# Shared weight loads, 16-head softmax groups, x stationary and TensorE in written order in a decode attention kernel

## The chip, the cores and the metric

One core of one Trainium2 chip. The metric is the device time of one execution in microseconds (us), median of several executions; "span" is the profiled execution without its fixed start and end, 1.6 to 1.8 us shorter. In the profiles, PE is TensorE's matmuls and PEld its weight loads (the weights are a matmul's stationary operand), DVE is VectorE, ACT is ScalarE, POOL is GpSimd and SP is SyncE, which here only issues transfers. "Clock" is the share of TensorE's full clock that was granted. `A <- B` in a list of waits means that A waited for B; `[0.30 <-B]` in a timeline means that the engine had been idle for 0.30 us, until B ended.

## The reference

```python
def reference(A_x, A_k_cache, A_v_cache, A_wq, A_wo, B_x, B_w_r, B_w_gate, B_w_up, B_w_down, gate_w):
    x = A_x                                          # (4, 1, 1024) bf16
    g = sigmoid((x * gate_w).sum(-1, keepdims=True))
    q = (x @ wq) as (4, 32 heads, 1, 128)
    p = softmax(q @ k_cache^T * 128 ** -0.5)         # k_cache, v_cache: (4, 32, 8192, 128) bf16
    a = (p @ v_cache) as (4, 1, 4096) @ wo
    b = x + sigmoid(x @ w_r) * ((silu(x @ w_gate) * (x @ w_up)) @ w_down)   # S = 1: the selection picks the only row
    return g * a + (1 - g) * b
```

(Shortened; the shapes are those of the inputs.) The K and V caches are 537 MB of the 576 MB that must be read.

## The kernel before

Each "piece" is 4 MB of K or V, or up to 4 MB of weights, loaded into one slot of a ring of five. Each K piece holds two heads and has four chunks; a chunk is transposed by DVE into one of two T buffers and then read by eight matmuls. A V piece feeds 32 matmuls. (In the code below and in the diffs, comments are added.)

```python
    ring = ctx.enter_context(tc.tile_pool(name="ring", bufs=5))
    ttp = ctx.enter_context(tc.tile_pool(name="ttp", bufs=2))      # the two T buffers
    ptp = ctx.enter_context(tc.tile_pool(name="ptp", bufs=2))
    # ... (cut)
    def add_x():                                    # adds (1 - g) * x into the output's accumulator
        xb = ptp.tile([Bn, D], BF, name="xb", bufs=1)
        nc.sync.dma_start(out=xb[:], in_=x2)
        xf = ptp.tile([Bn, D], F32, name="xf", bufs=1)
        nc.vector.tensor_copy(out=xf[:], in_=xb[:])
        for n in range(NH):
            mm_acc(acc[:, n * NB:(n + 1) * NB], dg[:], xf[:, n * NB:(n + 1) * NB])
    # ... (cut)
    def k_piece(u):
        # ... (cut)
        kn = slot()
        nc.sync.dma_start(out=kn[:], in_=kv_view(A_k_cache, u))
        for c in range(JR // CJ):
            T = ttp.tile([P, CJ, 2, 32, 2], BF, name="T", tag="T")
            nc.vector.transpose(out=T[:]...bitcast(U32), in_=kn[:, c * CJ * Dh:(c + 1) * CJ * Dh].bitcast(U32))
            for jl in range(CJ // 16):
                # ... (cut)
                for he in range(4):
                    nc.tensor.matmul(sps[:, :], lhsT=Z[:, he, s:s + P], rhs=T[:, 16 * jl:16 * jl + 16, half, :, e], ...)
            if c == 0:
                flush()
        if t == GT - 1:
            softmax(g)                              # GT = 4 pieces, 8 heads
    # ... (cut)
    for kind, u in order:                           # k 0, k 1, ..., then k u and v u - LAG in turn
        if kind == "k":
            k_piece(u)
        # ... (cut)
        if (kind, u) == ("k", NT // 2):             # NT // 2 = 32
            add_x()
```

Of the kernel before, what the change touches and what calls it, by code (L numbers as in the profile page):

```python
# [9 lines left out]
BF = mybir.dt.bfloat16  # L10
# [5 lines left out]
PSUM = bass.MemoryType.PSUM  # L16


@with_exitstack
def kernel(  # L20
# [21 lines left out]

    nc = tc.nc
# [8 lines left out]
    GT = 4  # L52
    GH = GT * HT
    NQ = 4
# [3 lines left out]
    LAG = 4  # L58
# [6 lines left out]
    assert JR == 128 and JC * GT == 32 and H % GH == 0 and D % NB == 0  # L65
# [7 lines left out]
    ptp = ctx.enter_context(tc.tile_pool(name="ptp", bufs=2))  # L73
    stat = ctx.enter_context(tc.tile_pool(name="stat", bufs=3))
    shrp = ctx.enter_context(tc.tile_pool(name="shrp", bufs=1, space=PSUM))
    accp = ctx.enter_context(tc.tile_pool(name="accp", bufs=1, space=PSUM))
    scp = ctx.enter_context(tc.tile_pool(name="scp", bufs=2, space=PSUM))
    ops = ctx.enter_context(tc.tile_pool(name="ops", bufs=2, space=PSUM))
    o2p = ctx.enter_context(tc.tile_pool(name="o2p", bufs=1, space=PSUM))

# [5 lines left out]
    x6 = const.tile([NX, D], BF)  # L86
# [5 lines left out]
    shr = shrp.tile([P, 512], F32)  # L92
    nc.vector.memset(shr[:], 0.0)
# [4 lines left out]
    xw_ps = o2p.tile([P, DT, NX], BF, name="xw", tag="oT")  # L98
# [7 lines left out]
    for he in range(4):  # L106
# [6 lines left out]
                            base=0, pattern=[[-JC, GT], [-32, NQ]], channel_multiplier=1)  # L113
    nc.gpsimd.affine_select(out=m32[:], in_=m32[:], compare_op=ALU.is_ge, fill=0.0,
                            base=JC - 1, pattern=[[JC, GT], [32, NQ]], channel_multiplier=-1)
# [6 lines left out]
    selg = const.tile([P, 4, GT, HT], F32)  # L122
    nc.gpsimd.memset(selg[:], 0.0)
    nc.gpsimd.affine_select(out=selg[:], in_=selg[:], compare_op=ALU.not_equal, fill=1.0,
                            base=0, pattern=[[-1, 4], [-32, GT], [-4, HT]], channel_multiplier=1)
    OS = [const.tile([P, 4 * Dh], F32, name=f"OS{i}") for i in range(2)]
    ZW = 31 + P + 1
    Zt = [const.tile([P, 4, ZW], BF, name=f"Z{i}") for i in range(2)]
    PB = [const.tile([P, 32, 4, HT, 4], BF, name=f"PB{i}") for i in range(2)]
    for z in Zt + PB + OS:  # L130
        nc.gpsimd.memset(z[:], 0.0)

    qT = const.tile([P, H, Bn], BF)
# [7 lines left out]
    FT = FG * FR  # L141
    o0 = 0
    gu_ps = shr[:, o0:o0 + 2 * FT * Bn].rearrange("p (w g r b) -> p w g r b", w=2, g=FG, r=FR); o0 += 2 * FT * Bn
    q_ps = shr[:, o0:o0 + H * Bn].rearrange("p (h b) -> p h b", h=H); o0 += H * Bn
    rg_ps = shr[:, o0:o0 + 2 * Bn].rearrange("p (w b) -> p w b", w=2); o0 += 2 * Bn
    assert o0 <= 512
    acc = accp.tile([Bn, D], F32)

# [6 lines left out]
    def gates():  # L155
        wrep = ttp.tile([P, 2, DT, P], BF, name="wrep", tag="T")
        for i in range(2):
            nc.vector.tensor_copy(out=wrep[:, i, :, :], in_=xw[:, :, Bn + i:Bn + i + 1].to_broadcast([P, DT, P]))
            for t in range(DT):
                mm_acc(rg_ps[:, i, :], wrep[:, i, t, :], xT[t])  # L160
        nc.scalar.activation(out=sgb[:], in_=rg_ps, func=ACT.Sigmoid)
# [4 lines left out]
    def add_x():  # L166
        xb = ptp.tile([Bn, D], BF, name="xb", bufs=1)
        nc.sync.dma_start(out=xb[:], in_=x2)
        xf = ptp.tile([Bn, D], F32, name="xf", bufs=1)
        nc.vector.tensor_copy(out=xf[:], in_=xb[:])  # L170
        for n in range(NH):
            mm_acc(acc[:, n * NB:(n + 1) * NB], dg[:], xf[:, n * NB:(n + 1) * NB])
# [8 lines left out]

    def wq_piece(t0):
        w = slot()[:, :TW * H * Dh].rearrange("p (t h d) -> p t h d", t=TW, h=H)
        nc.sync.dma_start(out=w.rearrange("p t h d -> p t (h d)"), in_=wqv[:, t0:t0 + TW, :])
        for t in range(TW):
            for h in range(H):
                mm_acc(q_ps[:, h, :], w[:, t, h, :], xT[t0 + t])

    def q_done():
        nc.vector.tensor_copy(out=qT[:], in_=q_ps)  # L190
        qa_ps = ops.tile([P, 4, H * Bn], F32, name="o_ps")
# [5 lines left out]
    def gu_piece(view, w_i, t0):  # L197
        w = slot()[:, :TW * F].rearrange("p (t g f r) -> p t g f r", t=TW, g=FG, r=FR)
        nc.sync.dma_start(out=w.rearrange("p t g f r -> p t (g f r)"), in_=view[:, t0:t0 + TW, :])
        for t in range(TW):  # L200
            for g in range(FG):
                for r in range(FR):
                    mm_acc(gu_ps[:, w_i, g, r, :], w[:, t, g, :, r], xT[t0 + t])

    def h_done():
        g_sb = stat.tile([P, FT, Bn], F32, tag="g_sb", bufs=1)
        fl = lambda ap: ap.rearrange("p g r b -> p (g r) b")
        nc.scalar.activation(out=g_sb[:], in_=fl(gu_ps[:, 0]), func=ACT.Silu)
# [60 lines left out]
    def k_piece(u):  # L269
# [3 lines left out]
        for a in range(NQ):  # L273
            nc.gpsimd.tensor_copy(out=Z[32 * a:32 * a + 32, :, 31 + 32 * a:32 + 32 * a],  # L274
# [160 lines left out]
```

## Time and profile before

| | before |
|---|---|
| time, median | 1351.3 us (1351.1 to 1351.8) |
| span | 1349.5 us |
| PE, PEld, DVE busy | 1066, 434, 623 us |
| data moved | 576.5 MB, mean 427 GB/s |

From the page of the kernel before: the span in 40 slices (busy tenths of PE and DVE, of the 16 DMA engines, and the rate of the transfers), the instruction queue (packets, MB, share), and the median time from issue to landing of a K piece.

```profile
PE   2775887888788877879788887879877787887878
DVE  1553445444553555355355435535553454455500
DMA  9999999999999999999999999999999999999997
GB/s 398 436 431 424 432 430 429 431 434 432 429 432 432 432 427 432 433 432 429 431 434 431 429 430 435 432 428 432 430 434 425 434 434 432 429 428 435 433 421 321
...
q8 instruction: 40, 0.66, 0.2%
...
piece<-in_A_k_cache_dram SPq DMA_DIRECT2D x64, 4096.0 KB, 37.4
```

DMA is at nine tenths or more in all slices but the last, whatever PE and DVE do. A piece lands 37.4 us after its issue, and 4 MB at 431 GB/s (an inner slice) take 9.7 us: nearly four pieces are typically queued. While that is so, idle PE or DVE costs nothing.

From the timeline of the same run, SP alone (start, duration, what): the issues around the middle, where the 8 KB of `x` for the residual (`xb`) are loaded.

From the timeline (start, duration, what): the last chunk of a K piece and a V piece on PE, and the end of the run.

```profile
641.22 1.90 PE L290 MATMUL S_ps<-T,Z_140 128*128 128x512 bf16 x8 [0.30 <-DVE T L283]
643.05 7.07 PE L346 MATMUL o_ps<-piece,PB_142 128*8 128x512 bf16 x32
...
1342.79 3.77 PE L150 MATMUL acc<-piece,LT 128*4 128x512 bf16 x16 [0.68 <-DMA piece<-in_A_wo_dram]
```

After the last piece of `wo` has landed there are 16 matmuls, a cast and the store. (One such matmul is shown as 0.38 us long when alone, yet 16 end within 3.77 us: matmuls overlap. This matters below.)

### The profile page before, as it was taken

How to read it: one execution, taken by the hardware profiler on the slowest of the kernel's cores; microseconds unless marked ns; L12 is line 12 of the kernel's file. 1: busy time of each engine (PE TensorE's matmuls, PEld its weight loads, DVE VectorE, ACT ScalarE, POOL GpSimd, SP SyncE). 2: the span in 40 equal slices, each digit the busy share in tenths (PEclk: the TensorE clock that was granted, in tenths of full speed). 3: DMA queues.
4: the chain of work that ended last, by engine and by line, in shares of the span. 5: the costliest groups of instructions: out<-in, count | busy, mean ns of one | idle time of the engine just before them, and what ended most of it. 6: DMA issues, size and time to landing. Idle time of an engine off the chain costs nothing.

```text
span 1349.5 us, 11806 instructions
## 1 busy us (share of the span) xinstructions
PE 1066.2 (79%) x5112; PEld 434.1 (32%) x5112; DVE 622.5 (46%) x403; ACT 71.0 (5%) x118; POOL 86.3 (6%) x326
## 2 busy tenths in 40 slices
PE   2775887888788877879788887879877787887878
PEld 2332333333233333323333333333333332333333
DVE  1553445444553555355355435535553454455500
ACT  0001000000000000000000000000000000000000
POOL 2000000000000000000000000000000000000000
PEclk9877998889898888979999888999989889998999
DMA  9999999999999999999999999999999999999997
GB/s 398 436 431 424 432 430 429 431 434 432 429 432 432 432 427 432 433 432 429 431 434 431 429 430 435 432 428 432 430 434 425 434 434 432 429 428 435 433 421 321
DMA packets 22040, 576.46 MB, mean 427 GB/s; under 512 B 2386, under 2 KB 2394, under 8 KB 2660
## 3 DMA queue, kind: packets, MB, share of 16 engines
q1 hardware_dynamic: 21968, 575.69, 99.4%
q8 instruction: 40, 0.66, 0.2%
q14 instruction: 12, 0.10, 0.0%
q10 hardware_dynamic: 20, 0.02, 0.0%
HBM read 575.69 MB, written 0.01 MB: 427 GB/s over the span
## 4 chain that ended last, share of the span: by engine, by line
DMA 48%; PE 32%; DVE 12%; issue 6%; POOL 2%; ACT 1%; DVEq 0%; SPq 0%; ACTq 0%
DMA piece<-in_A_k_cache_dram 42%; PE o_ps L346 16%; PE S_ps L290 14%; DVE T L283 10%; DMA piece<-in_A_v_cache_dram 5%; DMA piece<-in_A_wo_dram 1%; PE oT L359 1%; PE acc L150 1%; DVE PT L315 1%; PE shr L150 1%; POOL PB_142 L320 1%; POOL PB_143 L320 1%; POOL tot L324 0%; ACT OS_138 L352 0%; ACT OS_139 L352 0%
## 5 line engine op out<-in xcount | busy, mean ns | idle before, releaser
L283 DVE STREAM_TRANSPOSE T<-piece 128x2048 uint32<-128x2048 uint32 x256 | 576.2, 2288 | 455.9 <-DMA piece<-in_A_k_cache_dram 367.7
L290 PE MATMUL S_ps<-T,Z_140 128*128 128x512 bf16 x1024 | 288.9, 437 | 158.4 <-DVE T L283 158.1
L290 PE MATMUL S_ps<-T,Z_141 128*128 128x512 bf16 x1024 | 260.0, 402 | 81.5 <-DVE T L283 81.4
L346 PE MATMUL o_ps<-piece,PB_143 128*8 128x512 bf16 x1024 | 229.5, 383 | 4.6 <-DMA piece<-in_A_v_cache_dram 4.6
L346 PE MATMUL o_ps<-piece,PB_142 128*8 128x512 bf16 x1024 | 226.2, 379 | 4.1 <-DMA piece<-in_A_v_cache_dram 4.1
L290 PEld LDWEIGHTS <-Z_140 128*128 128x128 bf16 x1024 | 111.3, 109 | 332.5 <-issue 252.5
L290 PEld LDWEIGHTS <-Z_141 128*128 128x128 bf16 x1024 | 102.4, 101 | 237.9 <-issue 142.2
L346 PEld LDWEIGHTS <-PB_143 128*8 128x8 bf16 x1024 | 87.1, 87 | 143.2 <-issue 17.7
L346 PEld LDWEIGHTS <-PB_142 128*8 128x8 bf16 x1024 | 86.4, 87 | 141.6 <-issue 12.8
L362 DVE SCALAR_TENSOR_TENSOR OT<-oT,sgb,rinv 128x8 bf16<-128x8 f32 x16 | 3.8, 236 | 147.5 <-PE oT L359 147.5
L274 POOL COPY Z_141<-qa 32x4 bf16<-32x4 bf16 x128 | 24.9, 195 | 517.3 <-PE S_ps L290 511.8
L274 POOL COPY Z_140<-qa 32x4 bf16<-32x4 bf16 x128 | 24.9, 195 | 499.1 <-PE S_ps L290 485.1
L352 ACT COPY OS_138<-o_ps 8x512 f32<-8x512 f32 x32 | 18.5, 577 | 568.6 <-PE o_ps L346 568.6
L352 ACT COPY OS_139<-o_ps 8x512 f32<-8x512 f32 x32 | 18.5, 577 | 548.8 <-PE o_ps L346 548.8
L150 PE MATMUL shr<-xw,piece 128*128 128x4 bf16 x704 | 22.6, 170 | 2.8 <-DMA piece<-in_A_wq_dram 2.6
L150 PEld LDWEIGHTS <-piece 128*128 128x128 bf16 x704 | 22.6, 113 | 3.9 <-DMA piece<-in_A_wq_dram 2.7
L326 DVE RECIPROCAL rinv<-tot 128x8 f32<-128x8 f32 x16 | 3.2, 203 | 25.6 <-POOL tot L324 25.6
L150 PE MATMUL acc<-piece,LT 128*4 128x512 bf16 x64 | 14.5, 378 | 0.7 <-DMA piece<-in_A_wo_dram 0.7
L359 PE MATMUL oT<-selg,OS_139 128*128 128x8 f32 x64 | 8.5, 259 | 5.7 <-ACT OS_139 L352 5.7
L359 PE MATMUL oT<-selg,OS_138 128*128 128x8 f32 x64 | 8.5, 259 | 5.7 <-ACT OS_138 L352 5.7
L150 PE MATMUL acc<-piece,hT 128*4 128x512 bf16 x56 | 12.4, 379 | 0.0
L313 ACT ACTIVATE PTs<-S_ps,negm 128x512 bf16<-128x512 f32 x16 | 11.0, 688 | 25.8 <-DVE negm L310 25.4
(99 smaller groups left out, 142.5 us busy)
## 6 DMA issues: line engine op xcount, KB each, us to landing
piece<-in_A_k_cache_dram SPq DMA_DIRECT2D x64, 4096.0 KB, 37.4
piece<-in_A_v_cache_dram SPq DMA_DIRECT2D x63, 4096.0 KB, 36.2
piece<-in_A_wq_dram SPq DMA_DIRECT2D x2, 4096.0 KB, 22.6
piece<-in_B_w_gate_dram SPq DMA_DIRECT2D x2, 3584.0 KB, 39.9
piece<-in_B_w_up_dram SPq DMA_DIRECT2D x2, 3584.0 KB, 33.6
piece<-in_A_wo_dram SPq DMA_DIRECT2D x7, 1024.0 KB, 19.9
piece<-in_B_w_down_dram SPq DMA_DIRECT2D x1, 4096.0 KB, 39.7
piece<-in_A_v_cache_dram SPq DMA_DIRECT2D x4, 1024.0 KB, 31.7
```

The lines of the kernel that those rows point to most:

```text
L150: nc.tensor.matmul(out_ap, lhsT=lhsT, rhs=rhs, start=start, stop=True, skip_group_check=True)
L274: nc.gpsimd.tensor_copy(out=Z[32 * a:32 * a + 32, :, 31 + 32 * a:32 + 32 * a], in_=qa[32 * a:32 * a + 32, :, h0 + a // QH, b:b + 1])
L283: nc.vector.transpose(out=T[:].rearrange("p j h i e -> p (j h i e)").bitcast(U32), in_=kn[:, c * CJ * Dh:(c + 1) * CJ * Dh].bitcast(U32))
L290: nc.tensor.matmul(sps[:, :], lhsT=Z[:, he, s:s + P], rhs=T[:, 16 * jl:16 * jl + 16, half, :, e], start=(t == 0 and jc == 0 and he == 0), ...
L313: nc.scalar.activation(out=PTs[:], in_=sps[:], func=ACT.Exp, bias=negm[:, 0:1], scale=scale, accum_out=rs[:, 0:1])
L315: nc.vector.transpose(out=PT[:].rearrange("p j i -> p (j i)"), in_=PTs[:])
L320: nc.gpsimd.tensor_copy(out=B_[W:P, :, :, 1, :], in_=Pv[W:P])
L326: nc.vector.reciprocal(out=rinv[:], in_=tot[:])
L346: nc.tensor.matmul(o_ps[32 * t:32 * t + NM, :], lhsT=B_[:, JC * t + jc, uq].rearrange("p s j -> p (s j)"), rhs=vn[:, j0 * Dh:(j0 + 4) * Dh ...
L352: nc.scalar.copy(out=o_sb[32 * t:32 * t + NM, :], in_=o_ps[32 * t:32 * t + NM, :])
L359: nc.tensor.matmul(oT[:, :], lhsT=o_sb[:, q * Dh:(q + 1) * Dh], rhs=selg[:, q].rearrange("p t s -> p (t s)"), start=(q == 0), stop=(q == 3))
L362: nc.vector.scalar_tensor_tensor(out=OT[:, hg:hg + GH, b], in0=oT[:, :], scalar=sgb[:, 1, b:b + 1], in1=rinv_t.pop(g)[:], op0=ALU.mult, op ...
```

## The change

The intent: order the matmuls so that two in a row use the same weights, and drop the second weight load; form softmax groups of 16 heads (8 pieces) instead of 8, so that the pairs exist; compute q, gate and up with x as the stationary operand; keep TensorE's instructions in written order, so that pairs stay together. The larger tiles need room, so several small tiles move into other tiles' buffers. The core of the diff:

```diff
+def keep_weights(nc):        # drops a weight load equal to the one held, if it carries no wait or update
+    ...
-    GT = 4
+    GT = 8
-    LAG = 4
+    LAG = GT
-    ptp = ctx.enter_context(tc.tile_pool(name="ptp", bufs=2))
+    ptp = ctx.enter_context(tc.tile_pool(name="ptp", bufs=1))
-    scp = ctx.enter_context(tc.tile_pool(name="scp", bufs=2, space=PSUM))
+    scp = ctx.enter_context(tc.tile_pool(name="scp", bufs=1, space=PSUM))     # scores: one buffer, two banks
+    ctx.enter_context(tc.manual_schedule(engines={mybir.EngineType.PE}))
+    nc.at_finalize(keep_weights)
... (cut)
     def add_x():
-        xb = ptp.tile([Bn, D], BF, name="xb", bufs=1)
-        nc.sync.dma_start(out=xb[:], in_=x2)
-        xf = ptp.tile([Bn, D], F32, name="xf", bufs=1)
-        nc.vector.tensor_copy(out=xf[:], in_=xb[:])
+        xs = ttp.tile([Bn, 3 * D], BF, name="xs", tag="T")
+        xb, xf = xs[:, 0:D], xs[:, D:3 * D].bitcast(F32)
+        nc.sync.dma_start(out=xb, in_=x2)
+        nc.vector.tensor_copy(out=xf, in_=xb)
... (cut: q, gate and up with x stationary and transposes after them)
-            for jl in range(CJ // 16):
-                jc = c * (CJ // 16) + jl
-                s = 31 - (JC * t + jc)
-                for he in range(4):
-                    half, e = divmod(he, 2)
-                    nc.tensor.matmul(sps[:, :], lhsT=Z[:, he, s:s + P], rhs=T[:, 16 * jl:16 * jl + 16, half, :, e], ...)
+            s = 31 - (JT * t + c)
+            for he in range(4):
+                half, e = divmod(he, 2)
+                for z in range(2):
+                    nc.tensor.matmul(sps[:, z, :], lhsT=Z[:, he, s:s + P], rhs=T[:, 16 * z:16 * z + 16, half, :, e], ...)
... (cut: V likewise, pairs of matmuls with one weight load; eviction of four V pieces at a time by ACT and DVE)
     last += [wo_block(NWB - 1, 0, FR - 1), wo_block(NWB - 1, FR - 1, FR)]
+    last.pop(0)()
     flush()
+    last.pop(0)()
     o_rows(GE, NWB)
```

More of the change, by code (lines that the diff above doesn't have):

```diff
@@ L16 @@
 PSUM = bass.MemoryType.PSUM
+def keep_weights(nc):
+    for f in nc.m.functions:
+        for block in f.blocks:
+            held, kept, alone = None, [], False
+            for i in block.instructions:
+                if i.engine == mybir.EngineType.PE:
+                    if isinstance(i, mybir.InstLdweights):
+                        a, y = i.ins[0], i.sync_info
+                        key = (a.memref, a.offset, str(a.ap), str(a.dtype), i.tile_size, i.tile_position, i.is_transpose)
+                        free = y is None or not (y.on_wait or y.on_update)
+                        if free and held == key:
+                            continue
+                        held = key
+                    elif not isinstance(i, mybir.InstMatmult) or i.ldweights is not False:
+                        held = None
+                kept.append(i)
+            block.instructions = kept
 @with_exitstack
@@ L51 @@
     JC = JR // 16
-    GT = 4
+    GT = 8
+    JT = JC // 2
+    RT = 4
     GH = GT * HT
+    RH = RT * HT
     NQ = 4
@@ L64 @@
     assert Sq == 1 and Dh == P and D % P == 0 and F % (P * FR) == 0
-    assert JR == 128 and JC * GT == 32 and H % GH == 0 and D % NB == 0
+    assert H == 32 and JR == 128 and JT * GT == 32 and GT % RT == 0 and H % GH == 0 and D % NB == 0
     scale = float(Dh) ** -0.5
@@ L72, with small @@
     ttp = ctx.enter_context(tc.tile_pool(name="ttp", bufs=2))
-    ptp = ctx.enter_context(tc.tile_pool(name="ptp", bufs=2))
-    stat = ctx.enter_context(tc.tile_pool(name="stat", bufs=3))
-    shrp = ctx.enter_context(tc.tile_pool(name="shrp", bufs=1, space=PSUM))
+    ptp = ctx.enter_context(tc.tile_pool(name="ptp", bufs=1))
+    stat = ctx.enter_context(tc.tile_pool(name="stat", bufs=2))
     accp = ctx.enter_context(tc.tile_pool(name="accp", bufs=1, space=PSUM))
-    scp = ctx.enter_context(tc.tile_pool(name="scp", bufs=2, space=PSUM))
-    ops = ctx.enter_context(tc.tile_pool(name="ops", bufs=2, space=PSUM))
-    o2p = ctx.enter_context(tc.tile_pool(name="o2p", bufs=1, space=PSUM))
+    scp = ctx.enter_context(tc.tile_pool(name="scp", bufs=1, space=PSUM))
+    mps = ctx.enter_context(tc.tile_pool(name="mps", bufs=2, space=PSUM))
+    ctx.enter_context(tc.manual_schedule(engines={mybir.EngineType.PE}))
+    nc.at_finalize(keep_weights)
+    def small(shape, dtype=F32):
+        return mps.tile(shape, dtype, name="small", tag="small")
     def slot():
@@ L85 @@
     NX = Bn + 2
-    x6 = const.tile([NX, D], BF)
+    x6 = ttp.tile([NX, D], BF, name="x6", tag="T")
     nc.scalar.dma_start(out=x6[0:Bn], in_=x2)
@@ L89 @@
     nc.scalar.dma_start(out=x6[Bn + 1:Bn + 2], in_=gate_w.rearrange("(o n) -> o n", o=1))
-    shr = shrp.tile([P, 512], F32)
-    nc.vector.memset(shr[:], 0.0)
+    acc4 = accp.tile([P, 2, 512], F32)
+    o_ps = accp.tile([P, 2, 512], F32)
+    q_ps = scp.tile([P, 2, 512], F32, name="S_ps")
+    for z in (q_ps, o_ps, acc4):
+        nc.vector.memset(z[:], 0.0)
+    acc = acc4[0:Bn].rearrange("p z n -> p (z n)")
     ident = const.tile([P, P], F32)
@@ L97 @@
     nc.vector.tensor_copy(out=identb[:], in_=ident[:])
-    xw_ps = o2p.tile([P, DT, NX], BF, name="xw", tag="oT")
+    xw_ps = small([P, DT, NX], BF)
     for t in range(DT):
@@ L112 @@
     nc.gpsimd.affine_select(out=m32[:], in_=m32[:], compare_op=ALU.is_ge, fill=0.0,
-                            base=0, pattern=[[-JC, GT], [-32, NQ]], channel_multiplier=1)
+                            base=0, pattern=[[-JT, GT], [-32, NQ]], channel_multiplier=1)
     nc.gpsimd.affine_select(out=m32[:], in_=m32[:], compare_op=ALU.is_ge, fill=0.0,
-                            base=JC - 1, pattern=[[JC, GT], [32, NQ]], channel_multiplier=-1)
+                            base=JT - 1, pattern=[[JT, GT], [32, NQ]], channel_multiplier=-1)
     mask8 = const.tile([P, GH], F32)
@@ L121 @@
     nc.vector.tensor_scalar(out=nmask8[:], in0=mask8[:], scalar1=-scale, scalar2=None, op0=ALU.mult)
-    selg = const.tile([P, 4, GT, HT], F32)
+    selg = const.tile([P, 4, RT, HT], F32)
     nc.gpsimd.memset(selg[:], 0.0)
-    nc.gpsimd.affine_select(out=selg[:], in_=selg[:], compare_op=ALU.not_equal, fill=1.0,
-                            base=0, pattern=[[-1, 4], [-32, GT], [-4, HT]], channel_multiplier=1)
-    OS = [const.tile([P, 4 * Dh], F32, name=f"OS{i}") for i in range(2)]
+    for e in range(2):
+        nc.gpsimd.affine_select(out=selg[:], in_=selg[:], compare_op=ALU.not_equal, fill=1.0,
+                                base=-8 * e, pattern=[[-1, 4], [-32, RT], [-4, HT]], channel_multiplier=1)
+    mE4 = const.tile([P, 2, 4], F32)
+    nc.gpsimd.memset(mE4[:], 1.0)
+    nc.gpsimd.affine_select(out=mE4[:], in_=mE4[:], compare_op=ALU.is_ge, fill=0.0,
+                            base=0, pattern=[[-8, 2], [-32, 4]], channel_multiplier=1)
+    nc.gpsimd.affine_select(out=mE4[:], in_=mE4[:], compare_op=ALU.is_ge, fill=0.0,
+                            base=7, pattern=[[8, 2], [32, 4]], channel_multiplier=-1)
+    mE = const.tile([P, 2], F32)
+    nc.vector.tensor_reduce(out=mE[:], in_=mE4[:], axis=AX.X, op=ALU.add)
+    mq = const.tile([P, 1, NQ], BF)
+    nc.gpsimd.memset(mq[:], 1.0)
+    nc.gpsimd.affine_select(out=mq[:], in_=mq[:], compare_op=ALU.is_ge, fill=0.0,
+                            base=0, pattern=[[0, 1], [-32, NQ]], channel_multiplier=1)
+    nc.gpsimd.affine_select(out=mq[:], in_=mq[:], compare_op=ALU.is_ge, fill=0.0,
+                            base=31, pattern=[[0, 1], [32, NQ]], channel_multiplier=-1)
     ZW = 31 + P + 1
     Zt = [const.tile([P, 4, ZW], BF, name=f"Z{i}") for i in range(2)]
-    PB = [const.tile([P, 32, 4, HT, 4], BF, name=f"PB{i}") for i in range(2)]
-    for z in Zt + PB + OS:
+    PB = [const.tile([P, 32, 2, 2, 2, HT, 4], BF, name=f"PB{i}") for i in range(2)]
+    for z in Zt + PB:
         nc.gpsimd.memset(z[:], 0.0)
+    OS = const.tile([P, 4 * Dh], F32)
     qT = const.tile([P, H, Bn], BF)
@@ L139 @@
     c12 = const.tile([P, 2, Bn], F32)
-    FT = FG * FR
-    o0 = 0
-    gu_ps = shr[:, o0:o0 + 2 * FT * Bn].rearrange("p (w g r b) -> p w g r b", w=2, g=FG, r=FR); o0 += 2 * FT * Bn
-    q_ps = shr[:, o0:o0 + H * Bn].rearrange("p (h b) -> p h b", h=H); o0 += H * Bn
-    rg_ps = shr[:, o0:o0 + 2 * Bn].rearrange("p (w b) -> p w b", w=2); o0 += 2 * Bn
-    assert o0 <= 512
-    acc = accp.tile([Bn, D], F32)
     def mm_acc(out_ap, lhsT, rhs, start=False):
@@ L155, in gates @@
     def gates():
+        rg_ps = small([P, 2, Bn])
         wrep = ttp.tile([P, 2, DT, P], BF, name="wrep", tag="T")
@@ L159, in gates @@
             for t in range(DT):
-                mm_acc(rg_ps[:, i, :], wrep[:, i, t, :], xT[t])
-        nc.scalar.activation(out=sgb[:], in_=rg_ps, func=ACT.Sigmoid)
+                nc.tensor.matmul(rg_ps[:, i, :], lhsT=wrep[:, i, t, :], rhs=xT[t], start=(t == 0), stop=(t == DT - 1))
+        nc.scalar.activation(out=sgb[:], in_=rg_ps[:], func=ACT.Sigmoid)
         nc.vector.tensor_scalar(out=c12[:, 0, :], in0=sgb[:, 1, :], scalar1=-1.0, scalar2=1.0, op0=ALU.mult, op1=ALU.add)
@@ L180, with x_rows @@
     TW = 4
-    def wq_piece(t0):
-        w = slot()[:, :TW * H * Dh].rearrange("p (t h d) -> p t h d", t=TW, h=H)
-        nc.sync.dma_start(out=w.rearrange("p t h d -> p t (h d)"), in_=wqv[:, t0:t0 + TW, :])
-        for t in range(TW):
-            for h in range(H):
-                mm_acc(q_ps[:, h, :], w[:, t, h, :], xT[t0 + t])
-    def q_done():
-        nc.vector.tensor_copy(out=qT[:], in_=q_ps)
-        qa_ps = ops.tile([P, 4, H * Bn], F32, name="o_ps")
+    def x_rows(ps, w, t0, nb):
+        for t in range(TW):
+            for k in range(4):
+                for z in range((nb - k + 3) // 4):
+                    i = 4 * z + k
+                    nc.tensor.matmul(ps[32 * k:32 * k + Bn, z, :], lhsT=xT[t0 + t], rhs=w[:, t, i * NB:(i + 1) * NB],
+                                     start=(t0 + t == 0), stop=(t0 + t == DT - 1), skip_group_check=True)
+    def wq_piece(t0):
+        w = slot()[:, :TW * H * Dh].rearrange("p (t n) -> p t n", t=TW)
+        nc.sync.dma_start(out=w, in_=wqv[:, t0:t0 + TW, :])
+        x_rows(q_ps, w, t0, H * Dh // NB)
+    def q_done():
+        qs = ttp.tile([P, 2, 4, P], BF, name="qs", tag="T")
+        nc.vector.tensor_copy(out=qs[:].rearrange("p z c d -> p z (c d)"), in_=q_ps[:])
+        qt = small([P, 2, 4, 4, 32], BF)
+        for z in range(2):
+            for c in range(4):
+                nc.tensor.transpose(out=qt[:, z, c].rearrange("p k i -> p (k i)"), in_=qs[:, z, c, :], identity=identb[:])
+            nc.vector.tensor_copy(out=qT[:, 16 * z:16 * z + 16, :].rearrange("p (k c) b -> p c k b", c=4),
+                                  in_=qt[:, z, :, :, 0:Bn])
+        qa_ps = small([P, 4, H * Bn])
         for he in range(4):
@@ L197, in gu_piece @@
     def gu_piece(view, w_i, t0):
-        w = slot()[:, :TW * F].rearrange("p (t g f r) -> p t g f r", t=TW, g=FG, r=FR)
-        nc.sync.dma_start(out=w.rearrange("p t g f r -> p t (g f r)"), in_=view[:, t0:t0 + TW, :])
-        for t in range(TW):
-            for g in range(FG):
-                for r in range(FR):
-                    mm_acc(gu_ps[:, w_i, g, r, :], w[:, t, g, :, r], xT[t0 + t])
-    def h_done():
-        g_sb = stat.tile([P, FT, Bn], F32, tag="g_sb", bufs=1)
-        fl = lambda ap: ap.rearrange("p g r b -> p (g r) b")
-        nc.scalar.activation(out=g_sb[:], in_=fl(gu_ps[:, 0]), func=ACT.Silu)
-        nc.vector.tensor_tensor(out=g_sb[:], in0=g_sb[:], in1=fl(gu_ps[:, 1]), op=ALU.mult)
-        nc.vector.tensor_tensor(out=fl(hT[:]), in0=g_sb[:],
-                                in1=c12[:, 1:2, :].to_broadcast([P, FT, Bn]), op=ALU.mult)
+        w = slot()[:, :TW * F].rearrange("p (t n) -> p t n", t=TW)
+        nc.sync.dma_start(out=w, in_=view[:, t0:t0 + TW, :])
+        x_rows((o_ps, acc4)[w_i], w, t0, FG)
+    def h_done():
+        h = ttp.tile([P, 2, 512], F32, name="h", tag="T")
+        nc.scalar.activation(out=h[:], in_=o_ps[:], func=ACT.Silu)
+        nc.vector.tensor_tensor(out=h[:], in0=h[:], in1=acc4[:], op=ALU.mult)
+        for z in range(2):
+            ht = small([P, FR, 4, 32])
+            for r in range(FR):
+                nc.tensor.transpose(out=ht[:, r].rearrange("p k i -> p (k i)"), in_=h[:, z, r:512:FR], identity=ident[:])
+            kn = min(4, FG - 4 * z)
+            for r in range(FR):
+                nc.vector.tensor_tensor(out=hT[:, 4 * z:4 * z + kn, r, :], in0=ht[:, r, 0:kn, 0:Bn],
+                                        in1=c12[:, 1:2, :].to_broadcast([P, kn, Bn]), op=ALU.mult)
     def wd_piece(g0, ng):
@@ L228, in o_rows @@
         n = g1 - g0
-        lp = ops.tile([P, FR, n, Bn], F32, name="o_ps")
+        lp = small([P, FR, n, Bn])
         for k in range(WB):
@@ L272, in k_piece @@
         Z = Zt[u % 2]
-        for a in range(NQ):
-            nc.gpsimd.tensor_copy(out=Z[32 * a:32 * a + 32, :, 31 + 32 * a:32 + 32 * a],
-                                  in_=qa[32 * a:32 * a + 32, :, h0 + a // QH, b:b + 1])
+        nc.gpsimd.tensor_tensor(out=Z[:, :, 31:31 + P].rearrange("p e (s d c) -> p e s d c", s=HT, d=QH)[:, :, :, :, 0],
+                                in0=qa[:, :, h0:h0 + HT, b:b + 1].to_broadcast([P, 4, HT, QH]),
+                                in1=mq[:].rearrange("p o (s d) -> p o s d", s=HT).to_broadcast([P, 4, HT, QH]), op=ALU.mult)
         if t == 0:
-            S_ps[g] = scp.tile([P, 512], F32, name="S_ps")
+            S_ps[g] = scp.tile([P, 2, 512], F32, name="S_ps")
         sps = S_ps[g]
@@ L284, in k_piece @@
                                 in_=kn[:, c * CJ * Dh:(c + 1) * CJ * Dh].bitcast(U32))
-            for jl in range(CJ // 16):
-                jc = c * (CJ // 16) + jl
-                s = 31 - (JC * t + jc)
-                for he in range(4):
-                    half, e = divmod(he, 2)
-                    nc.tensor.matmul(sps[:, :], lhsT=Z[:, he, s:s + P], rhs=T[:, 16 * jl:16 * jl + 16, half, :, e],
-                                     start=(t == 0 and jc == 0 and he == 0),
-                                     stop=(t == GT - 1 and jc == JC - 1 and he == 3))
+            s = 31 - (JT * t + c)
+            for he in range(4):
+                half, e = divmod(he, 2)
+                for z in range(2):
+                    nc.tensor.matmul(sps[:, z, :], lhsT=Z[:, he, s:s + P], rhs=T[:, 16 * z:16 * z + 16, half, :, e],
+                                     start=(t == 0 and c == 0 and he == 0),
+                                     stop=(t == GT - 1 and c == JT - 1 and he == 3))
             if c == 0:
@@ L300, in softmax @@
         m1 = stat.tile([P, 1], F32, tag="m1")
-        nc.vector.tensor_reduce(out=m1[:], in_=sps[:], axis=AX.X, op=ALU.max)
+        nc.vector.tensor_reduce(out=m1[:], in_=sps[:].rearrange("p z n -> p (z n)"), axis=AX.X, op=ALU.max)
         mex = stat.tile([P, GH], F32, tag="mex")
@@ L310, in softmax @@
         nc.vector.tensor_reduce(out=negm[:], in_=gmm[:], axis=AX.X, op=ALU.add)
-        PTs = ptp.tile([P, 512], BF, name="PTs")
+        PTs = ptp.tile([P, 1024], BF, name="PTs")
         rs = stat.tile([P, 1], F32, tag="rs")
-        nc.scalar.activation(out=PTs[:], in_=sps[:], func=ACT.Exp, bias=negm[:, 0:1], scale=scale, accum_out=rs[:, 0:1])
-        PT = ptp.tile([P, 16, 32], BF, name="PT")
+        nc.scalar.activation(out=PTs[:], in_=sps[:].rearrange("p z n -> p (z n)"), func=ACT.Exp, bias=negm[:, 0:1], scale=scale, accum_out=rs[:, 0:1])
+        PT = ptp.tile([P, 32, 32], BF, name="PT")
         nc.vector.transpose(out=PT[:].rearrange("p j i -> p (j i)"), in_=PTs[:])
@@ L317, in softmax @@
         W = P // HT
-        Pv = PT[:].rearrange("p (q j) i -> p i q j", q=4)
-        nc.scalar.copy(out=B_[0:W, :, :, 0, :], in_=Pv[0:W])
-        nc.gpsimd.tensor_copy(out=B_[W:P, :, :, 1, :], in_=Pv[W:P])
+        Pv = PT[:].rearrange("p (q j) i -> p i q j", j=4)
+        Bv = B_[:].rearrange("p i z w e s j -> p i (z w e) s j")
+        nc.scalar.copy(out=Bv[0:W, :, :, 0, :], in_=Pv[0:W])
+        nc.gpsimd.tensor_copy(out=Bv[W:P, :, :, 1, :], in_=Pv[W:P])
         rex = stat.tile([P, GH], F32, tag="rex")
@@ L327, in softmax @@
         rinv_t[g] = rinv
-    NM = 4 * HT
+    NM = 8 * HT
     def v_piece(u):
@@ L333, in v_piece @@
         g, t = divmod(u, GT)
+        row = 32 * (t % RT)
         B_ = PB[g % 2]
@@ L340, in v_piece @@
             nc.sync.dma_start(out=vn[:, lo:hi], in_=vv[:, lo:hi])
-        o_ps = ops.tile([P, 4 * Dh], F32, name="o_ps")
         n = 0
-        for jc in range(JC):
-            for uq in range(4):
-                j0 = 16 * jc + 4 * uq
-                nc.tensor.matmul(o_ps[32 * t:32 * t + NM, :], lhsT=B_[:, JC * t + jc, uq].rearrange("p s j -> p (s j)"),
-                                 rhs=vn[:, j0 * Dh:(j0 + 4) * Dh], start=(n == 0), stop=(n == JR // 4 - 1))
-                n += 1
-                if n == 8:
-                    flush()
-        o_sb = OS[g % 2]
-        nc.scalar.copy(out=o_sb[32 * t:32 * t + NM, :], in_=o_ps[32 * t:32 * t + NM, :])
-        if t < GT - 1:
-            return
+        for c in range(JT):
+            for z in range(2):
+                for w in range(2):
+                    for e in range(2):
+                        j0 = 32 * c + 16 * z + 8 * w + 4 * e
+                        nc.tensor.matmul(o_ps[row:row + NM, e, :],
+                                         lhsT=B_[:, JT * t + c, z, w].rearrange("p e s j -> p (e s j)"),
+                                         rhs=vn[:, j0 * Dh:(j0 + 4) * Dh], start=(n == 0), stop=(n == JR // 8 - 1),
+                                         skip_group_check=True)
+                    n += 1
+                    if n == 4:
+                        flush()
+        if t % RT < RT - 1:
+            return
+        o_sb = OS
+        nc.scalar.activation(out=o_sb[:], in_=o_ps[:, 0, :], func=ACT.Copy, scale=mE[:, 0:1])
+        nc.vector.scalar_tensor_tensor(out=o_sb[:], in0=o_ps[:, 1, :], scalar=mE[:, 1:2], in1=o_sb[:],
+                                       op0=ALU.mult, op1=ALU.add)
+        r0 = RH * (t // RT)
         def finish():
-            oT = o2p.tile([P, GH], F32, name="oT")
+            oT = small([P, RH])
             for q in range(4):
@@ L360, in finish @@
                                  rhs=selg[:, q].rearrange("p t s -> p (t s)"), start=(q == 0), stop=(q == 3))
-            hg = h0 + HT - GH
-            nc.vector.scalar_tensor_tensor(out=OT[:, hg:hg + GH, b], in0=oT[:, :], scalar=sgb[:, 1, b:b + 1],
-                                           in1=rinv_t.pop(g)[:], op0=ALU.mult, op1=ALU.mult)
+            hg = h0 + HT - RH
+            nc.vector.scalar_tensor_tensor(out=OT[:, hg:hg + RH, b], in0=oT[:, :], scalar=sgb[:, 1, b:b + 1],
+                                           in1=rinv_t[g][:, r0:r0 + RH], op0=ALU.mult, op1=ALU.mult)
         pending.append(finish)
@@ L372 @@
             lambda: (gu_piece(wuv, 1, TW), h_done()), lambda: wd_piece(0, 4), lambda: wd_piece(4, FG - 4)]
-    GE = NWB - GH // WB
+    GE = NWB - RH // WB
     order = []
-    for u in range(NT - GT):
+    for u in range(NT - 2):
         order += [("k", u)] + [("v", u - LAG)] * (u >= LAG)
-    n0 = NT - GT - LAG
-    order += [("k", NT - 4), ("k", NT - 3), ("v", n0), ("k", NT - 2), ("k", NT - 1)]
-    order += [("v", u) for u in range(n0 + 1, NT)]
+    order += [("k", NT - 2), ("k", NT - 1)] + [("v", u) for u in range(NT - 2 - LAG, NT)]
     for kind, u in order:
@@ L391 @@
             add_x()
-        if (kind, u) == ("v", NT - LAG):
+        if (kind, u) == ("v", NT - RT):
             o_rows(0, GE)
```

## The prediction

> **What bounds the kernel now: the transfers.** The page's strip shows the 16 DMA engines busy 9 tenths or more in 39 of 40 slices; 576.5 MB move at a mean of 427 GB/s. In windows of 10 us the DMA share is 0.95 to 1.07 from 10 to 1340 us, with no dip where PE stalls. In the trace's DMA records a 32 KB packet takes 1215 ns (median), so 16 engines give 431.5 GB/s. This agrees with the Trainium skill, "DMA: Bandwidth & Descriptors", section "Specifications", whose fabric ceiling is 435 GB/s. 575.7 MB at 431.5 GB/s are 1334 us (estimate from the packet time), against a span of 1349.5 us.
>
> PE's 79% and DVE's 46% are not the bound. A K piece lands 37 us after its issue while 4 MB need 9.7 us: nearly four of the five ring slots are always queued. A compute stall of some 25 us would be absorbed. The chain of waits names PE and DVE for 44% of the span, but only walks through slot releases that feed a full queue.
>
> Outside the transfers are the head (345 GB/s in the first 10 us, about 2 us lost) and the tail: the last w_o piece lands at 1342.75 us, then follow 16 matmuls (3.8 us), a cast (0.6 us) and the store: 6.8 us.
>
> **What the change does.**
> - Weight loads: the built programs have 4980 loads and 5046 matmuls before, 2272 and 4534 after. K takes 1.90 us per 8 matmuls (237 ns each), V 7.01 us per 32 (219 ns). I expect 215 ns each, some 50 us of PE work in all. PE busy from 1066 to about 980 us (930 to 1050). Not on the limiting path: worth 0.
> - q, gate, up with x stationary: 128 short matmuls (3.55 us) per w_q piece become 32 of 512 columns; at most 7 us by the V rate. Hidden under transfers of 9.7 us.
> - Softmax 8 times instead of 16, twice as wide, single-buffered scores; TensorE in written order. At a group end the exp now waits behind the eviction of the V piece before it: some 4 to 8 us of PE idle, 8 times, swallowed by the queue.
> - No data bytes change. The instruction queues' packets took 3.1 us of the mean engine; about 45% fewer instructions save some 1.2 us of DMA time. This is the one gain on the limiting path.
> - Tail: same order of w_o pieces; the last V group is evicted by one ACT plus one DVE operation instead of one ACT copy of 0.58 us: about +0.8 us, but before the last landing. After it again 16 matmuls and the store, about 6.5 us.
>
> **Predicted time:** 1350 us, 8 in 10 between 1346.5 and 1353.5 us. Faster by over 2%: 0.01; within 2%: 0.96; slower: 0.03.
>
> **What would show it.** Right: DMA share still 9 in 39 slices, mean 427 to 429 GB/s, K pieces landing 35 us or more after issue, last w_o landing near 1341.5 us, DVE busy 610 to 640 us, PE idle larger with the time unchanged. Steps wrong: PE busy not below 1050 us (loads were already hidden); pieces at group ends landing under 20 us after issue (slack used up).
>
> **What would make it wrong.** A stall at a group end of over 30 us, or the clock falling for long stretches because PE idles more: a pair of pieces at half clock needs about 28 us against 19.4 us of transfer. Or packets that become quicker with less PE traffic: then the time falls, by about 1% at most.

## More of the kernel before

SP issues all large loads, one after another, and waits in that order for the buffer that each load needs.

```profile
624.86 0.33 SPq L340 DMA_DIRECT2D piece<-in_A_v_cache_dram  x1
633.82 0.33 SPq L280 DMA_DIRECT2D piece<-in_A_k_cache_dram  x1
634.19 0.36 SPq L168 DMA_DIRECT2D xb<-in_A_x_dram  x1
641.20 0.35 SPq L340 DMA_DIRECT2D piece<-in_A_v_cache_dram  x1
650.15 0.33 SPq L280 DMA_DIRECT2D piece<-in_A_k_cache_dram  x1
```

`xb` has a buffer of its own, so it goes out 0.4 us after the piece before it and holds nothing up.

## The result, and the profile after

| | before | after |
|---|---|---|
| time, median | 1351.32 us (1351.14 to 1351.78, 4 runs) | 1361.44 us (1359.36 to 1362.61, 4 runs) |
| ratio, 95% interval | 1 | 1.0073 (1.0055 to 1.009) |
| span of the profiled run | 1349.5 us | 1357.7 us |
| PE, PEld, DVE busy | 1066, 434, 623 us | 1061, 232, 632 us |

A ratio is the mean time of one kernel's fast runs over that of the other's of the same rounds, so it is not quite the ratio of the medians. The class is "within 2%", as forecast, but the time is 8 us above the upper end of the stated range.

The same lines of the page after the change, with the two large matmul groups and their weight loads:

```profile
PE   3667779876988879886877769788787859887778
DVE  3555654545544455445354455445454445456000
DMA  9999999999999999997999999999999999999998
GB/s 406 427 431 430 431 431 432 431 430 432 430 430 432 431 432 431 433 430 342 385 432 433 431 427 431 431 429 430 432 432 432 432 431 431 432 430 430 431 426 338
...
q8 instruction: 27, 0.44, 0.1%
...
L344 PE MATMUL S_ps<-T,Z 128*128 128x512 bf16 x2048 | 549.6, 419 | 252.4 <-DVE T L338 241.9
L403 PE MATMUL o_ps<-piece,PB 128*16 128x512 bf16 x2048 | 455.0, 380 | 17.2 <-DMA piece<-in_A_v_cache_dram 17.2
...
piece<-in_A_k_cache_dram SPq DMA_DIRECT2D x64, 4096.0 KB, 39.1
```

There is one hole: slices 19 and 20 fall to 342 and 385 GB/s. Every other slice is as before. Windows of 4 us over the hole (after the stretch: PE, PEld, DVE, ACT, POOL busy, clock, DMA share, GB/s):

```profile
632.00:636.00 4.00, 0.00 (x0) 0.00 (x0) 1.36 (x2) 2.42 (x3) 1.98 (x2) 0.63 1.05 451
636.00:640.00 4.00, 1.04 (x3) 0.25 (x2) 3.61 (x3) 0.00 (x0) 0.36 (x1) 0.50 0.42 180
640.00:644.00 4.00, 4.00 (x16) 2.07 (x12) 2.43 (x2) 0.00 (x0) 0.00 (x0) 0.59 0.02 4
644.00:648.00 4.00, 3.33 (x16) 0.68 (x7) 3.31 (x3) 0.00 (x0) 0.00 (x0) 1.00 0.01 2
648.00:652.00 4.00, 4.00 (x15) 0.71 (x9) 0.68 (x1) 0.00 (x0) 0.26 (x1) 1.00 0.98 354
```

Summing 4 us times what each of the last four shares lacks of 1 gives 0.58 + 0.98 + 0.99 + 0.02 = 2.57, times 4 = 10.3 us without transfers. That covers the whole loss (the spans of the two profiled runs differ by 8.2 us). The two costliest of SP's waits between 560 and 690 us (total, times, longest), and its issues:

```profile
SPq L208 <- DVE T L338: 42.4, 1, 42.4
SPq L396 <- DVE T L338: 38.4, 4, 13.3
```

```profile
602.19 0.33 SPq L396 DMA_DIRECT2D piece<-in_A_v_cache_dram  x1
647.27 0.32 SPq L208 DMA_DIRECT2D xs<-in_A_x_dram  x1
647.64 0.35 SPq L335 DMA_DIRECT2D piece<-in_A_k_cache_dram  x1
648.05 0.42 SPq L396 DMA_DIRECT2D piece<-in_A_v_cache_dram  x1
648.51 0.43 SPq L335 DMA_DIRECT2D piece<-in_A_k_cache_dram  x1
```

L208 is the 8 KB load of `xs`. From 602 to 647 us SP issued nothing. When `xs` was out, four pieces went out within 1.8 us (the fourth, at 649.04 us, is not shown): their slots had been free. `xs` now lives in a T buffer. The buffer that it gets is free only when K piece 32 has been transposed and multiplied as far as its third chunk; and that piece itself was still in the queue when SP reached `xs`. The timeline between:

```profile
631.30 1.11 ACT L367 ACTIVATE PTs<-S_ps,negm 128x1024 bf16<-128x1024 f32 x1 [1.16 <-DVE negm L364]
...
636.39 0.25 DVE L381 RECIPROCAL rinv<-tot 128x16 f32<-128x16 f32 x1 [2.49 <-POOL tot L379]
636.56 4.44 DVE L338 STREAM_TRANSPOSE T<-piece 128x2048 uint32<-128x2048 uint32 x2
638.96 3.57 PE L344 MATMUL S_ps<-T,Z 128*128 128x512 bf16 x8 [9.55 <-DVE T L338]
...
647.91 1.90 PE L344 MATMUL S_ps<-T,Z 128*128 128x512 bf16 x8 [0.67 <-DVE T L338]
```

Piece 32 is the first of a softmax group. Its transposes stand on DVE behind the whole softmax of the group before, so they start at 636.56 us, and PE, idle for 9.55 us, takes up its matmuls at half clock (3.57 us for eight instead of 1.90). The Trainium skill, "DMA: Bandwidth & Descriptors", section "Anatomy of one DMA — SWDGE (gpsimd) path", says that DMA engines do not wait on semaphores and that any wait happens on the issuing sequencer before dispatch. (The section is about transfers issued by GpSimd; these are issued by SP.) The issues above agree: 45 us in which the issuer sits on one entry.

### The profile page after: what moved, and what is told of

It reads as the page before. It is cut to its first block, busy times and chain, and to the rows that moved or that the text cites. A ratio compares the mean times of both kernels' runs of the same rounds, so it can differ in the third digit from the quotient of the medians.

```text
span 1357.7 us, 8253 instructions
## 1 busy us (share of the span) xinstructions
PE 1061.2 (78%) x4600; PEld 231.9 (17%) x2412; DVE 631.8 (47%) x375; ACT 41.5 (3%) x46; POOL 48.1 (4%) x115
## 4 chain that ended last, share of the span: by engine, by line
DMA 49%; PE 31%; DVE 12%; issue 6%; POOL 1%; ACT 1%; SPq 0%; DVEq 0%; ACTq 0%
DMA piece<-in_A_k_cache_dram 42%; PE o_ps L403 15%; PE S_ps L344 14%; DVE T L338 10%; DMA piece<-in_A_v_cache_dram 5%; DMA piece<-in_A_wo_dram 1%; PE small L421 1%; POOL PB L375 1%; DVE PT L369 1%; ACT PTs L367 1%; ACT OS L413 1%; DVE OS L414 1%; PE acc L188 0%; POOL tot L379 0%; DVE m L355 0%
## 5 line engine op out<-in xcount | busy, mean ns | idle before, releaser
L344 PE MATMUL S_ps<-T,Z 128*128 128x512 bf16 x2048 | 549.6, 419 | 252.4 <-DVE T L338 241.9
L403 PE MATMUL o_ps<-piece,PB 128*16 128x512 bf16 x2048 | 455.0, 380 | 17.2 <-DMA piece<-in_A_v_cache_dram 17.2
L344 PEld LDWEIGHTS <-Z 128*128 128x128 bf16 x1024 | 108.5, 106 | 677.7 <-issue 674.7
L403 PEld LDWEIGHTS <-PB 128*16 128x16 bf16 x1024 | 91.6, 90 | 373.7 <-issue 361.9
L414 DVE SCALAR_TENSOR_TENSOR OS<-o_ps,mE,OS 128x512 f32<-128x512 f32 x16 | 12.0, 751 | 175.8 <-ACT OS L413 175.8
L328 POOL TENSOR_TENSOR Z<-qa,mq 128x16 bf16<-128x16 bf16 x64 | 16.8, 264 | 1084.7 <-PE S_ps L344 1067.0
L421 PEld LDWEIGHTS small<-selg,OS 128*128 128x128 f32 x128 | 22.9, 253 | 12.0 <-issue 11.1
L421 PE MATMUL small<-selg,OS 128*128 128x8 f32 x128 | 20.6, 288 | 0.0
L375 POOL COPY PB<-PT 64x1024 bf16<-64x1024 bf16 x8 | 15.1, 1889 | 28.8 <-DVE rex L377 28.8
L374 ACT COPY PB<-PT 64x1024 bf16<-64x1024 bf16 x8 | 15.3, 1909 | 10.6 <-DVE PT L369 10.6
## 6 DMA issues: line engine op xcount, KB each, us to landing
piece<-in_A_k_cache_dram SPq DMA_DIRECT2D x64, 4096.0 KB, 39.1
```

Source lines behind the costliest of these rows:

```text
L328: nc.gpsimd.tensor_tensor(out=Z[:, :, 31:31 + P].rearrange("p e (s d c) -> p e s d c", s=HT, d=QH)[:, :, :, :, 0], in0=qa[:, :, h0:h0 + HT ...
L344: nc.tensor.matmul(sps[:, z, :], lhsT=Z[:, he, s:s + P], rhs=T[:, 16 * z:16 * z + 16, half, :, e], start=(t == 0 and c == 0 and he == 0), ...
L374: nc.scalar.copy(out=Bv[0:W, :, :, 0, :], in_=Pv[0:W])
L375: nc.gpsimd.tensor_copy(out=Bv[W:P, :, :, 1, :], in_=Pv[W:P])
L403: nc.tensor.matmul(o_ps[row:row + NM, e, :], lhsT=B_[:, JT * t + c, z, w].rearrange("p e s j -> p (e s j)"), rhs=vn[:, j0 * Dh:(j0 + 4) * ...
L414: nc.vector.scalar_tensor_tensor(out=o_sb[:], in0=o_ps[:, 1, :], scalar=mE[:, 1:2], in1=o_sb[:], op0=ALU.mult, op1=ALU.add)
```

## The experiments

Three theories. Theory 1: `xs` at the head of SP's queue waits for a T buffer, and nothing behind it can be issued. Theory 2: the 16-head softmax with one score buffer stalls PE too long. Theory 3: `xs` takes one of two T buffers from the K path, which slows that piece. The first four runs shared one chip and the same runs of the kernel before (median 1351.24 us); so did the last four, on another chip (1351.31 us). So e5_k34, e6_noshare, e7_nosched and e8_ring3 are compared with e1_own across two chips, on which the kernel before differs by 0.1 us. All gave correct results.

### e1_own: xs in a buffer of its own

```diff
-        xs = ttp.tile([Bn, 3 * D], BF, name="xs", tag="T")
+        xs = ptp.tile([Bn, 3 * D], BF, name="xs")
```

> The changed kernel, with x for the residual (xs) in a buffer of its own instead of one of the two T buffers. Theory 1 (xs waits 42.4 us at the head of the transfer queue for a T buffer, and nothing behind it can be issued): the dip at 637 to 648 us goes, the wait of SP before xs is under 2 us, time 1350 us (1349 to 1351.5), a touch under before (about -1 us by fewer instruction fetches). Rival, theory 2 (the 16-head softmax with single-buffered scores stalls PE at group ends, and once it is too long): the dip stays, 1360 us. Theory 3 (xs takes one of two T buffers from the K path, which slows that piece): 1350 us as theory 1; the run with the ACT queue tells those two apart.

Measured: 1349.60 us (1349.47 to 1349.70, 5 runs), ratio to before 0.9987 (0.9974 to 0.9999). The rates over the slices, and the windows at the same group end:

```profile
GB/s 404 435 428 427 432 429 430 434 430 432 429 434 427 433 431 435 426 433 431 432 430 432 431 430 430 435 430 428 433 434 427 431 432 434 427 433 432 433 421 325
```

```profile
636.00:640.00 4.00, 0.02 (x1) 0.05 (x1) 2.59 (x3) 0.74 (x1) 1.27 (x2) 0.50 1.03 442
640.00:644.00 4.00, 4.00 (x12) 1.47 (x9) 2.99 (x3) 0.00 (x0) 0.00 (x0) 0.50 0.93 401
644.00:648.00 4.00, 4.00 (x13) 1.57 (x10) 2.02 (x2) 0.00 (x0) 0.00 (x0) 0.50 1.03 432
```

The hole is gone although PE still idles at the group end and even stays at half clock for the full 12 us. So the softmax by itself costs nothing here, and theory 2 falls. This version, and e3_actq with it, beats both kernels, though only by 1.6 us over the one before.

### e3_actq: xs still in a T buffer, issued by ACT

```diff
-        nc.sync.dma_start(out=xb, in_=x2)
+        nc.scalar.dma_start(out=xb, in_=x2)
```

> The changed kernel, with the load of xs issued from ACT's queue instead of SP's; still in a T buffer, still behind the softmax of piece 32. Theory 1: the pieces are issued past it, no dip, 1350 us (1349 to 1352); ACT waits some tens of us for the buffer with nothing else due. Theory 3 (the T buffer taken from the K path): the dip stays, 1357 us or more. Theory 2: 1360 us.

Measured: 1349.56 us (1349.53 to 1349.70, 5 runs), the same as e1_own, and no hole: 425 to 435 GB/s in all slices but the first and the last two. Where ACT issued it and who waited then:

```profile
648.79 0.26 ACTq L208 DMA_DIRECT2D xs<-in_A_x_dram  x1
655.05 0.68 DVE L209 CAST xs<-xs 4x1024 f32<-4x1024 bf16 x1 [5.68 <-DMA xs<-in_A_x_dram]
...
655.78 3.57 PE L188 MATMUL acc<-xs,dg 4*4 4x512 f32 x4 [4.47 <-DVE xs L209]
```

`xs` gets its T buffer as late as before (648.8 us), the K path loses the buffer all the same, and PE waits 4.47 us for it. None of this shows in the time. Theory 3 falls; what counts is in whose queue the wait stands.

### e4_beforeT: the kernel before, with xs in a T buffer

```diff
-        xb = ptp.tile([Bn, D], BF, name="xb", bufs=1)
-        nc.sync.dma_start(out=xb[:], in_=x2)
-        xf = ptp.tile([Bn, D], F32, name="xf", bufs=1)
-        nc.vector.tensor_copy(out=xf[:], in_=xb[:])
+        xs = ttp.tile([Bn, 3 * D], BF, name="xs", tag="T")
+        xb, xf = xs[:, 0:D], xs[:, D:3 * D].bitcast(F32)
+        nc.sync.dma_start(out=xb, in_=x2)
+        nc.vector.tensor_copy(out=xf, in_=xb)
```

> The kernel before, with this one thing of the change: xs in a T buffer. It says whether that alone makes the loss, without the 16-head groups, the shared weight loads and the written order. Theory 1: SP waits 40 to 50 us before xs, the queue runs dry for 4 to 10 us behind the 8-head softmax, time 1355 to 1361 us. Theory 2: no change, 1351 us.

Measured: 1360.43 us (1359.03 to 1361.98, 5 runs), 9.2 us over the kernel before. SP's wait before `xs`:

```profile
SPq L169 <- DVE T L283: 43.1, 1, 43.1
```

The rates fall to 401 and 324 GB/s in slices 20 and 21. This one edit makes nearly the whole loss, without shared loads, larger groups or written order.

### e2_mid and e5_k34: the add of x at other K pieces

```diff
-        if (kind, u) == ("k", NT // 2):
+        if (kind, u) == ("k", NT // 2 + GT // 2):        # e2_mid: piece 36
+        if (kind, u) == ("k", NT // 2 + 2):              # e5_k34: piece 34
```

> The changed kernel, with the add of x moved from K piece 32 (first of a group, behind a softmax) to K piece 36 (middle of a group); xs still in a T buffer, issued from SP. Theory 1 with the softmax as what lengthens it: SP still waits some 35 to 40 us before xs, but the piece that frees the buffer lands about 9.7 us before the queue runs dry and needs about 9 us of transpose and matmul, so DMA is idle for only 0.5 to 3 us: time 1350.5 to 1353 us. If the block alone costs it, whatever stands there: 1360 us. Theory 2 (softmax alone): 1360 us, dip still at 637 us.

> The changed kernel, with the add of x moved to K piece 34, which stands behind neither a softmax nor an eviction (piece 36 turned out to stand behind the eviction of V piece 27, and to meet PE at half clock: it cost 5 us, not the 0.5 to 3 foreseen). xs is still in a T buffer, issued from SP. Theory 1: SP waits about 33 to 36 us before xs, the queue runs dry for 1 to 4 us, time 1350.5 to 1353.5 us, between e1_own and e2_mid. If the place did not matter beyond the softmax: 1354.6 us as e2_mid.

Measured: e2_mid 1354.60 us (1354.18 to 1356.54, 5 runs), e5_k34 1353.25 us (1351.81 to 1354.26, 5 runs). Piece 36 was a miss in size: its expectation overlooked that it stands behind the eviction of four V pieces and meets PE at half clock. From e2_mid's timeline:

```profile
708.47 0.75 DVE L414 SCALAR_TENSOR_TENSOR OS<-o_ps,mE,OS 128x512 f32<-128x512 f32 x1 [9.71 <-ACT OS L413]
709.27 4.51 DVE L338 STREAM_TRANSPOSE T<-piece 128x2048 uint32<-128x2048 uint32 x2
711.63 3.57 PE L344 MATMUL S_ps<-T,Z 128*128 128x512 bf16 x8 [3.92 <-DVE T L338]
```

Piece 34 stands behind neither, and its median lies inside its range; but SP waited 28.1 us, less than the 33 to 36 us expected, and the transfers lost lie at or just over the upper end of the 1 to 4 us. The three places side by side, each from its profiled run; "DMA lost" is summed over 4 us windows around the dip as above (for piece 34, whose dip is shallow, from 668 to 688 us; its two deepest windows alone give 3.8 us), "over e1_own" is the profiled run's time less e1_own's 1349.51 us:

| xs at piece | SP's wait for DVE's T | DMA lost | over e1_own |
|---|---|---|---|
| 34 (plain) | 28.1 us | 4.6 us | 3.8 us |
| 36 (behind an eviction) | 35.8 us | 7.9 us | 7.0 us |
| 32 (behind a softmax) | 42.4 us | 10.3 us | 9.9 us |
| 32, own buffer | none | none | 0 |

The longer the freeing piece is held up, the longer the queue is dry, and nearly every dry microsecond shows in the time. What comes back (0.4 to 0.9 us) is no more than the choice of windows shifts, and was not followed up. The waits at pieces 34 and 36 cost time although they are shorter than the 39.1 us that a K piece takes from issue to landing: what counts is the work queued at that moment. After SP's last issue before `xs` the engines ran dry in some 29 us at piece 34, 36 us at piece 36 and 37 us at piece 32 (from windows of 0.5 us), and the next piece was issued after 30.8, 41.2 and 45.4 us. The excess is 2, 6 and 9 us; the loss is about 2 us more, for running out unevenly and starting again.

### e6_noshare: e1_own with every weight load kept

```diff
-    nc.at_finalize(keep_weights)
```

> e1_own with every weight load kept (4460 instead of 2272), order and all else as it was. If the loads were hidden already: PE busy 1063 us within 8, 8 matmuls of a K chunk still in 1.90 us, PEld busy 435 us; time only longer by the fetch of some 2190 more instructions, about 140 KB in the instruction queues, 0.3 to 1.0 us: 1349.9 to 1350.6 us. If sharing pays on PE: PE busy over 1080 us.

Measured: 1351.04 us (1350.98 to 1351.18, 5 runs), 1.4 us over e1_own: more than the 0.3 to 1.0 us expected. Its PE busy time is 1064 us, against 1063 us in e1_own. Its page:

```profile
q8 instruction: 36, 0.59, 0.2%
...
L343 PE MATMUL S_ps<-T,Z 128*128 128x512 bf16 x2048 | 550.4, 420 | 242.7 <-DVE T L337 231.3
...
L343 PEld LDWEIGHTS <-Z 128*128 128x128 bf16 x2048 | 212.6, 105 | 571.4 <-issue 397.5
```

2188 loads fewer give PE nothing: the matmul group takes 550.4 us with them and 548.6 us without (e1_own). What they give is fewer instructions to fetch, 0.59 MB against 0.44 MB in this queue. The last `wo` piece lands at 1342.53 us instead of 1341.00 us in e1_own, and the time follows. The fetch packets' time, averaged over the 16 engines, is only 0.6 us less, so the landing moved by some 2.7 times that. Fetches that fall unevenly on the engines might do this, if the last piece has to wait for the slowest of them; it was not tested.

### e7_nosched: e1_own with TensorE in the scheduler's order

```diff
-    ctx.enter_context(tc.manual_schedule(engines={mybir.EngineType.PE}))
```

> e1_own with TensorE's instructions in the scheduler's order instead of the written one. If the order is hidden under the transfers: 1349.6 us within 0.5. If the written order matters: over 1350.5 us, or under 1348.5 us.

Measured: 1350.70 us (1350.51 to 1351.06, 5 runs), 1.1 us over e1_own. The end on PE, in e7_nosched and then in e1_own:

```profile
1333.83 11.99 PE L187 MATMUL acc<-piece,LT 128*4 128x512 bf16 x47
```

```profile
1331.13 1.89 PE L188 MATMUL acc<-piece,LT 128*4 128x512 bf16 x8 [0.47 <-DMA piece<-in_A_wo_dram]
...
1333.94 1.89 PE L188 MATMUL acc<-piece,LT 128*4 128x512 bf16 x8
...
1341.04 3.79 PE L188 MATMUL acc<-piece,LT 128*4 128x512 bf16 x16 [0.59 <-DMA piece<-in_A_wo_dram]
```

In the scheduler's order 47 of the `wo` matmuls are left when the last head is done, and they run without a gap to 1345.8 us: there the end is bound by PE. The written order does two blocks of `wo` during the last eviction, so that PE is waiting again when the last piece lands, and ends 1.0 us earlier.

### e8_ring3: e1_own with three ring slots

```diff
-    ring = ctx.enter_context(tc.tile_pool(name="ring", bufs=5))
+    ring = ctx.enter_context(tc.tile_pool(name="ring", bufs=3))
```

> e1_own with three ring slots instead of five, so two pieces (19.4 us) queued behind the one in use instead of four. It tests that the depth of the queue is what hides the group ends. If so: DMA share dips behind every softmax, 8 times some 1 to 5 us, and behind PE at half clock, time 1353 to 1390 us, dips in the slices of group ends. If five slots were more than needed: 1350 us.

Measured: 1373.98 us (1367.11 to 1378.32, 4 runs), ratio to before 1.0163 (1.0136 to 1.019).

```profile
DMA  9999989999999999999999989999999998999998
GB/s 407 429 430 427 432 365 436 431 429 401 410 428 432 435 388 432 435 428 429 400 433 434 430 369 435 434 427 431 383 435 431 430 432 376 430 427 432 434 424 347
```

Seven dips, from slice 6 to slice 34, so 28 / 6 = 4.7 slices or 160 us apart. Eight pairs of pieces, one softmax group, take about 8 x 19.4 = 155 us of transfers: these are the group ends. (The first seven softmax groups reach their exp at 174, 326, 487, 644, 803, 965 and 1123 us in this trace, each in the slice of a dip or the one before it. Eight dips were expected; the eighth group, at 1266 us, has no K piece behind it and shows none.) They are there in e1_own too, and the depth of the queue hides them.

## Why the prediction was right or wrong

- **Bound by transfers: right.** All versions with a full queue lie within 1.8 us of each other, whatever PE does.
- **The step that failed** is "nearly four of the five ring slots are always queued. A compute stall of some 25 us would be absorbed." It took the full queue as given and asked only what compute may do to it. The change put a wait into the queue itself: the prediction's list of what moves ("No data bytes change") leaves out that the 8 KB of x moved into a T buffer. That entry waited 42.4 us, SP issued no piece for 45.4 us, the engines ran dry some 37 us into that, and 10.3 us of transfers were lost. The sign that the prediction named, K pieces landing 35 us or more after issue, held all the same (39.1 us): a median over 64 pieces does not show one hole. e4_beforeT shows that the edit alone does it, e1_own and e3_actq that without it the time is 1349.6 us, inside the predicted range and 0.4 us from its centre. The 8 us by which the range was missed is this term, sized at zero.
- **Softmax at group ends: right for the cost, low for the size.** "Some 4 to 8 us of PE idle" was 9.55 us at this group end (9.59 us in e1_own, where the queue swallowed it), but it lengthened the wait of `xs`: compare piece 34 with piece 32.
- **"Some 50 us of PE work in all": wrong.** PE busy is 1061 us, not 930 to 1050. The error was arithmetic: 1.90 us for eight matmuls was divided by eight, but one alone is shown as 0.38 us, so the spacing was already (1.90 - 0.38) / 7 = 0.217 us, and (7.07 - 0.38) / 31 = 0.216 us for V. The loads were hidden. This agrees with the Trainium skill, "TensorE: Matmul & The Clock Gate", section "Step-by-step: what each phase is for", which says that PE can pull weight loads ahead of running matmuls: in the trace of the kernel before, eight K loads (1.62 us) fall inside the 1.90 us of eight matmuls, and e6_noshare shows that they cost PE nothing.
- **x stationary, hidden under transfers: right, and cheaper than feared.** A `wq` piece takes 3.59 us, not up to 7: its 32 matmuls, which write to four groups of 32 partitions in turn, take 0.11 us each, half of V's 0.216 us. Why was not tested.
- **Instruction fetch "some 1.2 us": right in kind, its size in part luck.** e1_own is 1.6 us under before, and e6_noshare gives back 1.4 us. But the trace has 30% fewer instructions (11806 to 8253), not 45%, and the packets of the two instruction queues take 0.9 us less of the mean engine (3.1 to 2.2 us, summed from the trace). Fetch does not have the gain to itself either: e7_nosched gives back 1.1 us, so the two come to more than the 1.6 us, and what offsets them was not looked for.
- **Tail: right for the order of landings;** that the written order itself is worth 1.1 us there (e7_nosched) was not foreseen.

## What to carry to other kernels

In a kernel bound by transfers, read the queue of the engine that issues them as a critical resource: an entry that waits for a compute buffer, however small its load (8 KB here), stops the loads behind it, and costs roughly the time by which the pause in issuing exceeds the work queued at that moment (here plus some 2 us). When tiles are moved to save room, check for each load which buffer it now needs, what frees it, and whether what frees it is still in the same queue; if so, give it a buffer of its own or another issuing engine. And take the spacing of overlapping matmuls as (group's time - one matmul's) / (count - 1) before believing that weight loads cost anything.

## What the Trainium skill lacked or had wrong

- "DMA: Bandwidth & Descriptors" says where a transfer's wait is made, but neither there nor in its rules for authors that a waiting entry stops the loads behind it on the same issuer; nor does "Perfetto Trace Analysis" draw this from its timeline of such a transfer. Here one 8 KB load waited 42.4 us and left the DMA engines dry for 10.3 us; issued by ACT instead, it cost nothing (1349.56 us).
- "TensorE: Matmul & The Clock Gate", section "Back-to-back issue gap", gives some 131 ns per matmul of 512 columns in a stream of loads and matmuls, and calls its 216 ns an isolated gap. The K and V streams here run at 216 to 217 ns, with a load for every matmul (before) and for every second one (after). The page disagrees with itself: its section "Step-by-step: what each phase is for" has 216 ns as the back-to-back gap. Only the x-stationary matmuls, which write to four groups of 32 partitions in turn, are closer together (0.11 us).
- "Runtime: NRT & Kernel Launch", section "Instruction fetch mechanics", calls the cost of fetching instructions by DMA mostly hidden, and no page was found that prices its share of the DMA engines. 2188 weight loads more (10442 against 8254 instructions in the trace) cost 1.4 us in a kernel that is bound by transfers (e6_noshare).
